# mLSTM attention and two feed-forward layers: heads 4 to 7 with their batch halves swapped, the state's part of the output in the scores' burst, output in the pair banks, new planner offsets

## The chip, the cores and the metric

The kernel runs on one core of a Trainium2 chip. The metric is the time in device microseconds of one execution; several runs are taken and their median is compared. The engines are PE (matrix products; PEld is its weight load), DVE (VectorE), ACT (ScalarE), POOL (GpSimd) and SP (which issues the DMAs).

## The reference

Inputs: q, k, v and the output gate of shape (4 batches, 8 heads, 768 steps, 40), input and forget gates (4, 8, 768). All is computed in float32.

```
for t in range(S):                      # mLSTM, for each batch b and head h
    m_new = max(f[t] + m, i[t])
    f_s, i_s = exp(f[t] + m - m_new), exp(i[t] - m_new)
    C = f_s * C + i_s * outer(v[t], k[t])
    n = f_s * n + i_s * k[t]
    y[t] = sigmoid(o[t]) * (C @ q[t]) / max(abs(n . q[t]), 1)
x = y as (3072, 320)
x = leaky(x @ w_in1) @ w_out1           # 320 -> 2048 -> 320, slope 0.01
x = h * cos(h), h = x @ w_in2; out = that @ w_out2
```

## The kernel before

**Attention.** The 768 steps are cut into 12 spans of 64 (T), the four batches into two pairs, which gives 24 chunks in the order `ORDER` (span s, pair p). A chunk holds two batches (j = 0, 1), each on 64 of the 128 partitions, and 8 heads, h = 4 hh + a. `pair` is a PSUM tile of two banks. `a_scores` (L554) writes k times q into it: contraction over the 40 features on rows 64 hh, output rows 64 j, bank hh. `a_weigh` (L561) multiplies with the decay weights, which `a_scan` (L533) makes. `a_out` then issues three groups: q times the state into `pair` (L575, only for s > 0), weights times v into `po` (L583, contraction over the 64 steps on rows 64 j, output rows 64 j) and the state's update into `pair` (L591). `a_ys` (L619, L621) scales the state's part and adds it to `po`; `a_norm`, `a_scale` and `a_gate` (L642) make the chunk's output x from it. `po` is a bank of the ring `acc` (three banks) for chunks 0 to 3 and of the ring `tr` (one bank) afterwards. `a_kt` (L543) scales k for the update; `a_scores` is queued behind it. `g_turn` (L322, L327) turns the gates of several spans from rows to columns by small matmuls with the identity.

**Feed-forward.** Layer 0 runs over 8 blocks of 4, 2, 3, ... chunks of 128 tokens, layer 1 over 8 blocks of 3; each block has 16 slots, one for each 128 of the 2048 hidden features. A slot is 8 matmuls in (L710), an activation, a split into high and low parts (`gh`, `gl` at L758) and 3 matmuls per chunk out (L778). x is turned by the PE (`x_turn`, L469). Block 0 needs all of chunks 0 to 3. The weights arrive as 64-bit words (704 KB each) and are decoded: `w_bits` (L386), `w_round` (POOL), `w_mask` (L402), `w_hi` (ACT), `w_lo` (L417).

**Order.** A planner, `Schedule.run`, issues all work. Each task has a due time (`t_need` of the chunk or `t_slot` of the slot, less an offset from `OFF`), a cost, tasks that it depends on, and rings of buffers that it takes and frees; of the tasks that can start first on an engine it picks the one with the earliest due time. The resulting order is what each engine's queue holds; the planner's times aren't used on the chip. `g_busy` (L251) issues dummy matmuls in the first part.

Of the kernel before, what the change touches and what calls it, by code (L numbers as in the profile page):

```python
# [10 lines left out]
F32 = mybir.dt.float32  # L11
# [11 lines left out]
P = 128  # L23
# [13 lines left out]
KV = OO + DM  # L37
O_S, O_C = HD * E1, 2 * HD * E1
SR = T + D
# [11 lines left out]
SLOW = 50.0  # L51
T_START = 16.163
ATT_LEAD = 25.402
BACKLOG = 0.429
HORIZON = 180.0
ATT_GAP = 11.301
ATT_STEP = 13.206
OUT_LAG = 6.451
SLOT0 = 2.559
DEC_LEAD = 35.272  # L60
BUSY = [-1.11, 44.0, 0.7, -11.9]
SPREAD = 4
# [106 lines left out]
def mlstm_moe(ctx, tc, qk, kvo, ig, fg, w1, w2, const, out):  # L169
# [145 lines left out]
    def g_turn(eng, c0, c1):  # L315
        pt = bank() if c0 < 4 else tps.tile([P, 512], F32, tag="tr", name="pt")
        pt = pt[:, :(c1 - c0) * 6 * H]
        pt = pt_t[c0] = pt.rearrange("p (s k n) -> p s k n", k=3, n=2 * H)
        for s in range(c0, c1):
            for k, t in enumerate((gt["i"], gt["m"])):  # L320
                for j in range(2):
                    nc.tensor.matmul(  # L322
                        pt[T * j:T * j + T, s - c0, k, :].rearrange("p (b h) -> p b h", h=H), t[:, s * T:s * T + T],
                        ident[:BH, :BH].rearrange("r (b j h) -> r j b h", j=2, h=H)[:, j], start=True, stop=True, skip_group_check=True,
                    )
        for hh in range(2):
            nc.tensor.matmul(pt[T * hh:T * hh + T, :, 2, :], ones, pick[:, hh, c0:c1, :], start=True, stop=True, skip_group_check=True)  # L327

# [285 lines left out]

    def a_ys(eng, c):
        s, p = ORDER[c]
        y = ap.tile([P, 2, HD, E1], F32, tag="y", name="y", bufs=1)
        g = col[:, s, 1, p * H:(p + 1) * H].rearrange("p (k a) -> p k a", k=2).unsqueeze(3)
        nc.vector.tensor_tensor(y, s_ps.rearrange("p k (a e) -> p k a e", e=E1), g.to_broadcast([P, 2, HD, E1]), ALU.mult)  # L619
        po = at[c]["po"]  # L620
        nc.vector.tensor_tensor(po, po, y.rearrange("p k a e -> p (k a e)"), ALU.add)  # L621

    def a_norm(eng, c):
        if eng == "ACT":
            at[c]["d"] = ap.tile([P, H, 1], F32, tag="d", name="d")
        d = at[c]["d"]
        n = at[c]["po"].rearrange("p (h e) -> p h e", e=E1)[:, :, D:E1]
        if eng == "ACT":
            nc.scalar.activation(d, n, AF.Abs)
# [9 lines left out]
    def a_gate(eng, c):  # L639
        o = at[c]["kvo"][:, OO:].rearrange("p (h d) -> p h d", d=D)  # L640
        x = ap.tile([P, H, D], F32, tag="x", name="x")
        nc.vector.tensor_tensor(x, at[c]["po"].rearrange("p (h e) -> p h e", e=E1)[:, :, :D], o, ALU.mult)  # L642
        ax[c] = x.rearrange("p h d -> p (h d)")

    def plan_attention(n, c, j, m):
        s, p = ORDER[c]
        e = t_need[c]
        last, k = s == NS - 1, (0, c)
        c0 = max(c for c, _ in TURNS if c <= s)
# [16 lines left out]
        if not last:  # L666
            kt = [("kt", c)]
            sch.add(("kt", c), e - OFF["kt"], [pool(DM), dve(DM)], a_kt, c, deps=[("kvo", c), ("scan", c)])
        sch.add(("s", c), e - OFF["s"], ("PE", 0.72), a_scores, c, deps=[("qk", c, 0), ("qk", c, 1), ("scan", c), "clear"] + kt,
                take=[("p", (c, 0), (s > 0) + (not last)), ("p", (c, 1), (s > 0) + (not last))])  # L670
        sch.add(("weigh", c), e - OFF["weigh"], dvp(4 * P), a_weigh, c, deps=[("s", c), ("scan", c)] + kt)
        sch.add(("sig", c), e - OFF["sig"], ("ACT", 0.36), a_sig, c, deps=[("kvo", c), ("exp", 2, "f"), ("exp", 2, "i")], table="sig")
        sch.add(("out", c), e - OFF["out"], ("PE", 1.3 + (0.45 if s else 0) + (0.27 if not last else 0)), a_out, c,
                deps=[("weigh", c), ("vext", c)] + ([("state", c - 2)] if s else []) + kt
                + ([("col", TURNS[-1][0])] if c == BLOCKS1[0] else []),
                take=[(po_ring(c), ("po", c), 1)], free=[("fb", c), ("raw", c), ("kvo", c)])
        if s:
            sch.add(("ys", c), e - OFF["ys"], ("DVE", 0.82), a_ys, c, deps=[("out", c)], free=[("p", (c, 0)), ("p", (c, 1))])
        sch.add(("norm", c), e - OFF["norm"], ("ACT", 0.08), a_norm, c, deps=[("ys", c) if s else ("out", c)], take=[("d", c, 1)])
        sch.add(("rec", c), e - OFF["norm"], ("DVE", 0.3), a_norm, c, deps=[("norm", c)])  # L680
        sch.add(("scale", c), e - OFF["scale"], [pool(DM), dve(DM)], a_scale, c, deps=[("rec", c), ("sig", c)], free=[("d", c)])
        sch.add(("gate", c), e - OFF["gate"], dvp(DM), a_gate, c, deps=[("scale", c)], take=[("x", k, 1)],
                free=[(po_ring(c), ("po", c)), ("kvo", c)])
        if not last:
            if s:
                sch.add(("decay", c), t_need[c - 2] - OFF["decay"], [pool(H * E1), dve(H * E1)], a_decay, c, deps=[("state", c - 2), ("col", c0)],
                        take=[("tmp", c, 1)])
            sch.add(("state", c), e - OFF["state"], dvp(H * E1) if s else [("ACT", 0.35), dvp(H * E1)], a_state, c,
                    deps=[("out", c)] + ([("decay", c)] if s else []), free=[("p", (c, 0)), ("p", (c, 1))] + ([("tmp", c)] if s else []))
        plan_x(0, n, c, j, e - OFF["tr"], ("gate", c), ax, "x", m)  # L690
# [244 lines left out]
```

## Time and profile before

| what | value |
|---|---|
| runs | 830.17, 831.56, 831.58 us; median 831.56 |
| profiled execution | span 829.0 us from first to last instruction; no other time of its own is shown |
| busy | PE 813.4, PEld 781.0, DVE 602.0, ACT 430.8, POOL 85.4 us |
| first layer matmul | 55.25 us |

The span is the time between the first and last instruction of the profiled execution; what an execution spends around it is in the runs' times only. PE's busy time holds its dummy matmuls.

### The profile page before, as it was taken

To read this page: it belongs to the slowest core of one execution; us is meant where nothing else is said; L and a number is where in the kernel's file an instruction comes from. 1 tells how busy PE (TensorE), PEld (TensorE's weight loads), DVE (VectorE), ACT (ScalarE), POOL (GpSimd) and SP (SyncE) were. 2 spreads that over 40 slices of the span, in tenths; PEclk is the share of its full clock that TensorE was granted. 3 is DMA by queue.
4 is the path that set the end of the run, shared out by engine and by line. 5 is a ranking of instruction groups with operands and counts; after the bars stand their busy time and mean duration, and the time that the engine had idled before them with its cause. 6 is when DMAs were issued, how large, how long until landed. Compare 5 with 4: busy or idle time off the path is not lost.

```text
span 829.0 us, 19156 instructions
## 1 busy us (share of the span) xinstructions
PE 813.4 (98%) x7782; PEld 781.0 (94%) x7792; DVE 602.0 (73%) x1250; ACT 430.8 (52%) x925; POOL 85.4 (10%) x68
## 2 busy tenths in 40 slices
PE   7979999999999999999999999999999999999998
PEld 5758889999999999999999999999999999999998
DVE  7888875557465663665517798989898988888885
ACT  3456634443344344443344565656565666666564
POOL 2442311112111121100000000000000000000000
PEclk8599999999999999999999999999999999999999
DMA  8466354535243352643215300000000000010000
GB/s 240 157 206 180 118 144 136 163 119 171 88 156 109 135 167 85 190 127 125 77 51 165 113 25 17 25 25 25 25 25 25 25 17 33 9 32 17 9 17 25
DMA packets 29976, 74.55 MB, mean 90 GB/s; under 512 B 4353, under 2 KB 13697, under 8 KB 29889
## 3 DMA queue, kind: packets, MB, share of 16 engines
q1 hardware_dynamic: 29888, 73.33, 28.5%
q8 instruction: 61, 1.00, 0.5%
q14 instruction: 27, 0.21, 0.1%
HBM read 59.60 MB, written 13.71 MB: 88 GB/s over the span
## 4 chain that ended last, share of the span: by engine, by line
PE 91%; DVE 3%; ACT 0%; issue 0%
PE acc L778 41%; PE ph L710 36%; PE pair L710 6%; PE po L583 2%; PE tr L469 2%; PE pair L554 2%; PE pair L575 1%; DVE w L417 1%; PE pair L591 1%; DVE wf L402 0%; ACT w L199 0%; PE busy L251 0%; DVE r L735 0%; DVE g L746 0%; DVE y L619 0%
## 5 line engine op out<-in xcount | busy, mean ns | idle before, releaser
L778 PE MATMUL acc<-w,gh 128*128 128x320 f32 x1568 | 348.0, 309 | 0.0
L710 PE MATMUL ph<-xt,w 128*128 128x384 f32 (+2 forms) x1760 | 344.1, 338 | 0.1
L710 PEld LDWEIGHTS ph<-xt,w 128*128 128x128 f32 x1760 | 297.2, 188 | 5.7 <-PE busy L251 0.6
L778 PEld LDWEIGHTS acc<-w,gh 128*128 128x128 f32 x1568 | 264.2, 188 | 2.5
L778 PE MATMUL acc<-w,gl 128*128 128x320 f32 (+1 forms) x784 | 238.7, 308 | 0.0
L758 DVE TENSOR_TENSOR gl<-ph,gh 128x384 fp32r<-128x384 f32 (+2 forms) x124 | 68.6, 553 | 115.3 <-ACT ph L719 115.0
L718 ACT ACTIVATE gh<-ph 128x384 fp32r<-128x384 f32 (+2 forms) x124 | 60.9, 491 | 166.9 <-PE ph L710 124.2
L778 PEld LDWEIGHTS acc<-w,gl 128*128 128x128 f32 x784 | 145.9, 188 | 0.3 <-DVE gl L758 0.2
L740 ACT ACTIVATE r<-r,hpi 128x384 f32<-128x384 f32 x128 | 78.9, 616 | 61.9 <-DVE r L736 61.7
L199 ACT CAST gh<-g 128x384 fp32r<-128x384 f32 x128 | 65.7, 513 | 46.1 <-PE acc L778 37.8
L398 POOL TENSOR_TENSOR wf<-wf,raw 128x704 int32<-128x704 int32 x32 | 60.7, 1897 | 270.8 <-DVE wf L386 143.1
L758 DVE TENSOR_TENSOR gl<-g,gh 128x384 fp32r<-128x384 f32 x128 | 70.5, 550 | 5.5 <-ACT gh L199 5.5
L746 DVE TENSOR_TENSOR g<-ph,r 128x384 f32<-128x384 f32 x96 | 53.4, 556 | 15.4 <-ACT r L740 14.1
L719 ACT ACTIVATE ph<-ph 128x384 f32<-128x384 f32 (+2 forms) x124 | 60.3, 486 | 0.0
L710 PE MATMUL pair<-xt,w 128*128 128x384 f32 x288 | 56.1, 337 | 1.1 <-DVE g L746 1.1
L726 ACT ACTIVATE t<-ph 128x384 f32<-128x384 f32 x96 | 47.0, 489 | 17.1 <-PE ph L710 11.2
L735 DVE SCALAR_TENSOR_TENSOR r<-t,ph 128x384 f32<-128x384 f32 x96 | 53.2, 555 | 3.3
L732 DVE TENSOR_SCALAR t<-t 128x384 f32<-128x384 f32 x128 | 45.7, 357 | 12.0 <-ACT t L726 8.4
L710 PEld LDWEIGHTS pair<-xt,w 128*128 128x128 f32 x288 | 49.4, 188 | 1.4 <-DVE g L746 1.4
L736 DVE TENSOR_SCALAR r<-r 128x384 f32<-128x384 f32 x128 | 46.1, 360 | 4.4
L199 ACT CAST xt<-tr 128x256 fp32r<-128x256 f32 x96 | 25.2, 316 | 17.0 <-PE tr L469 17.0
L417 DVE TENSOR_TENSOR w<-wf,w 128x704 fp32r<-128x704 f32 x32 | 32.5, 1016 | 1.7 <-ACT w L199 1.1
(93 smaller groups left out, 666.4 us busy)
## 6 DMA issues: line engine op xcount, KB each, us to landing
raw<-w SPq DMA_DIRECT2D x32, 704.0 KB, 5.9
kvo<-kvo SPq DMA_DIRECT2D x24, 484.0 KB, 4.6
raw<-qk SPq DMA_DIRECT2D x48, 192.0 KB, 4.7
w2d<-wf SPq DMA_DIRECT2D x16, 352.0 KB, 2.5
wf<-w2d SPq DMA_DIRECT2D x16, 352.0 KB, 3.2
fb<-sfd SPq DMA_DIRECT2D x40, 128.0 KB, 3.5
x2d<-o SPq DMA_DIRECT2D x24, 160.0 KB, 1.8
x<-x2d SPq DMA_DIRECT2D x24, 160.0 KB, 2.2
```

Of the source, the lines that this page charges most:

```text
L199: nc.scalar.copy(dst, src)
L398: nc.gpsimd.tensor_tensor(f, f, wraw.pop((l, i))[:, :, 0], ALU.add)
L710: nc.tensor.matmul(ph[:, :N], w[:, a:a + P], x[:, b, :N], start=k == 0, stop=k == 7)
L718: nc.scalar.activation(t["gh"][:, :N], h, AF.Prelu, alpha=0.01)
L719: nc.scalar.activation(h, h, AF.Prelu, alpha=0.01)
L726: nc.scalar.activation(t["a"][:, :N], t["h"][:, :N], AF.Copy, scale=1.0 / TWO_PI, bias=0.25)
L735: nc.vector.scalar_tensor_tensor(r, a, -TWO_PI, t["h"][:, :N], ALU.mult, ALU.add)
L736: nc.vector.tensor_scalar(r, r, -4.712388, 1.5707959, ALU.max, ALU.min)
L740: nc.scalar.activation(r, r, AF.Sin, bias=hpi)
L746: nc.vector.tensor_tensor(t["g"][:, :N], t["h"][:, :N], t["r"][:, :N], ALU.mult)
L758: on[eng].tensor_tensor(t["gl"][:, :N], t["g"][:, :N], t["gh"][:, :N].bitcast(F32), ALU.subtract)
L778: nc.tensor.matmul(po, a[:, s], w[:, b, e], start=i == 0 and k == 0 and j < 3, stop=i == NF - 1 and k == 2, skip_group_check=True,)
```

## The change

In q, k, v and the gates, heads 4 to 7 lie with the two batches of a pair exchanged, so that their steps of batch j stand on the partitions of batch 1 - j; the output gate stays. Matmuls of these heads write to the rows of their true batch. The weights times v go to `ps[hh]`: for chunks 0 to 3 two banks of `acc`, afterwards the two banks of `pair`. The state's part is issued in `a_scores`, to other columns of `pair`, and scaled by a new task `ym`. From chunk 4 on the banks of `pair` are freed by the weighing, the state's update and the gate. Turning the gates takes more and smaller matmuls. The planner's constants are new.

```diff
-O_S, O_C = HD * E1, 2 * HD * E1
+O_C, O_S = HD * E1, 512 - HD * E1
...
-T_START = 16.163
-ATT_LEAD = 25.402
+T_START = 26.475
+ATT_LEAD = 18.152
...
-ATT_GAP = 11.301
-ATT_STEP = 13.206
...
-DEC_LEAD = 35.272
+ATT_GAP = 9.276
+ATT_STEP = 10.696
...
+DEC_LEAD = 34.492
...
 OFF = {
-    "fb": 117.132, "kvo": 14.305, "qk": 13.373, "vext": 0.206, "scan": 113.123, "kt": -27.683, "s": -1.889, "weigh": 134.356, "out": 1.728,
-    "sig": 41.602, "ys": 144.171, "norm": -42.558, "scale": 136.89, "gate": 112.746, "state": 61.378, "decay": 54.572, "tr": 61.443,
-    "x2": 16.215, "l_a": -78.384, "l_g": -57.167, "l_cos": 77.728, "l_mul": 3.513, "l_gh": 58.007,
-    "l_gl": 101.205, "w_round": -66.41, "w_mask": 45.509, "w_hi": -52.232, "w_lo": 103.697, "w_load": -9.735,
+    "fb": 59.294, "kvo": 22.296, "qk": 24.167, "vext": 132.922, "scan": 113.856, "kt": 8.959, "s": 5.345, "weigh": 26.276, "out": -2.716,
+    "sig": 60.18, "ym": 66.406, "ys": 123.389, "norm": 36.865, "scale": 27.072, "gate": 48.573, "state": 80.334, "decay": 116.597, "tr": -11.831,
+    "x2": 16.236, "l_a": 22.842, "l_g": -40.025, "l_cos": 6.259, "l_mul": 80.975, "l_gh": 87.277,
+    "l_gl": -78.065, "w_round": 13.341, "w_mask": 35.707, "w_hi": -24.26, "w_lo": -27.626, "w_load": -7.818,
...
-            for k, t in enumerate((gt["i"], gt["m"])):
-                for j in range(2):
+            for j in range(2):
+                nc.tensor.matmul(
+                    pt[T * j:T * j + T, s - c0, 0, :].rearrange("p (b h) -> p b h", h=H), gt["i"][:, s * T:s * T + T],
+                    ident[:BH, :BH].rearrange("r (b j h) -> r j b h", j=2, h=H)[:, j], start=True, stop=True, skip_group_check=True,
+                )
+            for j in range(2):
+                for hh in range(2):
+                    r = T * (j ^ hh)
                     nc.tensor.matmul(
-                        pt[T * j:T * j + T, s - c0, k, :].rearrange("p (b h) -> p b h", h=H), t[:, s * T:s * T + T],
-                        ident[:BH, :BH].rearrange("r (b j h) -> r j b h", j=2, h=H)[:, j], start=True, stop=True, skip_group_check=True,
+                        pt[r:r + T, s - c0, 1, :].rearrange("p (b k a) -> p k b a", k=2, a=HD)[:, hh], gt["m"][:, s * T:s * T + T],
+                        ident[:BH, :BH].rearrange("r (b j k a) -> r j k b a", j=2, k=2, a=HD)[:, j, hh], start=True, stop=True,
+                        skip_group_check=True,
                     )
-        for hh in range(2):
-            nc.tensor.matmul(pt[T * hh:T * hh + T, :, 2, :], ones, pick[:, hh, c0:c1, :], start=True, stop=True, skip_group_check=True)
+        nc.tensor.matmul(pt[:T, :, 2, :], ones, pick[:, 0, c0:c1, :], start=True, stop=True, skip_group_check=True)
+        for j in range(2):
+            o, i = (x.rearrange("p s (b j a) -> p j s b a", j=2, a=HD) for x in (pt[T:, :, 2, :], pick[:, 1, c0:c1, :]))
+            nc.tensor.matmul(o[:, 1 - j], ones, i[:, j], start=True, stop=True, skip_group_check=True)
...
     def a_scores(eng, c):
+        s, p = ORDER[c]
         r = at[c]["raw"]
+        for a in range(HD if s else 0):
+            for hh in range(2):
+                for j in range(2):
+                    k, o = slice(T * hh, T * hh + D), T * (j ^ hh)
+                    nc.tensor.matmul(
+                        pair[o:o + T, hh, O_S + a * E1:O_S + (a + 1) * E1], r[k, 0, a * P + T * j:a * P + T * j + T],
+                        state[p][k, (j ^ hh) * HD + a, :], start=True, stop=True, skip_group_check=True,
                    )
...
+    def own_po(c):
+        return c < BLOCKS1[0]
+
+    def halves(x):
+        return x.rearrange("p (k h d) -> p k h d", k=2, h=HD)
 
     def a_out(eng, c):
         s, p = ORDER[c]
         t = at[c]
-        po = t["po"] = (bank() if po_ring(c) == "acc" else tps.tile([P, 512], F32, tag="tr", name="po"))[:, :H * E1]
-        if s:
-            for a in range(HD):
-                for hh in range(2):
-                    for j in range(2):
-                        k = slice(T * hh, T * hh + D)
-                        nc.tensor.matmul(
-                            pair[T * j:T * j + T, hh, O_S + a * E1:O_S + (a + 1) * E1],
-                            t["raw"][k, 0, a * P + T * j:a * P + T * j + T], state[p][k, j * HD + a, :],
-                            start=True, stop=True, skip_group_check=True,
-                        )
-        for h in range(H):
-            for j in range(2):
-                r = slice(T * j, T * j + T)
-                nc.tensor.matmul(
-                    po[r, h * E1:(h + 1) * E1], t["w"][r, h, :], t["v"][r, h, :], start=True, stop=True, skip_group_check=True,
-                )
+        if own_po(c):
+            ps = [bank()[:, :HD * E1] for _ in range(2)]
+            t["po"] = [(slice(k, k + 1), x.unsqueeze(1).rearrange("p k (h e) -> p k h e", e=E1)) for k, x in enumerate(ps)]
+        else:
+            ps = [pair[:, k, :HD * E1] for k in range(2)]
+            t["po"] = [(slice(0, 2), pair[:, :, :HD * E1].rearrange("p k (h e) -> p k h e", e=E1))]
+        for a in range(HD):
+            for hh in range(2):
+                for j in range(2):
+                    r, h, o = slice(T * j, T * j + T), hh * HD + a, T * (j ^ hh)
+                    nc.tensor.matmul(
+                        ps[hh][o:o + T, a * E1:(a + 1) * E1], t["w"][r, h, :], t["v"][r, h, :], start=True, stop=True, skip_group_check=True,
+                    )
         if s < NS - 1:
             for a in range(HD):
                 for j in range(2):
                     for hh in range(2):
                         r, h = slice(T * j, T * j + T), hh * HD + a
                         nc.tensor.matmul(
-                            pair[T * hh:T * hh + D, j, O_C + a * E1:O_C + (a + 1) * E1],
+                            pair[T * hh:T * hh + D, j ^ hh, O_C + a * E1:O_C + (a + 1) * E1],
...
-    def a_ys(eng, c):
+    def a_inter(eng, c):
         s, p = ORDER[c]
-        y = ap.tile([P, 2, HD, E1], F32, tag="y", name="y", bufs=1)
+        y = at[c]["y"] = ap.tile([P, 2, HD, E1], F32, tag="y", name="y", bufs=1)
         g = col[:, s, 1, p * H:(p + 1) * H].rearrange("p (k a) -> p k a", k=2).unsqueeze(3)
         nc.vector.tensor_tensor(y, s_ps.rearrange("p k (a e) -> p k a e", e=E1), g.to_broadcast([P, 2, HD, E1]), ALU.mult)
-        po = at[c]["po"]
-        nc.vector.tensor_tensor(po, po, y.rearrange("p k a e -> p (k a e)"), ALU.add)
+
+    def a_ys(eng, c):
+        y = at[c]["y"]
+        for k, po in at[c]["po"]:
+            nc.vector.tensor_tensor(po, po, y[:, k], ALU.add)
 
...
-        sch.add(("s", c), e - OFF["s"], ("PE", 0.72), a_scores, c, deps=[("qk", c, 0), ("qk", c, 1), ("scan", c), "clear"] + kt,
-                take=[("p", (c, 0), (s > 0) + (not last)), ("p", (c, 1), (s > 0) + (not last))])
-        sch.add(("weigh", c), e - OFF["weigh"], dvp(4 * P), a_weigh, c, deps=[("s", c), ("scan", c)] + kt)
+        sch.add(("s", c), e - OFF["s"], ("PE", 0.72 + (0.45 if s else 0)), a_scores, c,
+                deps=[("qk", c, 0), ("qk", c, 1), ("scan", c), "clear"] + kt + ([("state", c - 2)] if s else []),
+                take=[("p", (c, a), 1 + (not own) + (not last)) for a in range(2)])
+        if s:
+            sch.add(("ym", c), e - OFF["ym"], dvp(H * E1), a_inter, c, deps=[("s", c), ("col", c0)], take=[("y", c, 1)])
+        sch.add(("weigh", c), e - OFF["weigh"], dvp(4 * P), a_weigh, c, deps=[("s", c), ("scan", c)] + kt, free=pair_)
...
-        sch.add(("out", c), e - OFF["out"], ("PE", 1.3 + (0.45 if s else 0) + (0.27 if not last else 0)), a_out, c,
-                deps=[("weigh", c), ("vext", c)] + ([("state", c - 2)] if s else []) + kt
+        sch.add(("out", c), e - OFF["out"], ("PE", 0.72 + (0.27 if not last else 0)), a_out, c,
+                deps=[("weigh", c), ("vext", c)] + kt
                 + ([("col", TURNS[-1][0])] if c == BLOCKS1[0] else []),
-                take=[(po_ring(c), ("po", c), 1)], free=[("fb", c), ("raw", c), ("kvo", c)])
+                take=[("acc", ("po", c, a), 1) for a in range(2)] if own else [], free=[("fb", c), ("raw", c), ("kvo", c)])
         if s:
-            sch.add(("ys", c), e - OFF["ys"], ("DVE", 0.82), a_ys, c, deps=[("out", c)], free=[("p", (c, 0)), ("p", (c, 1))])
...
         sch.add(("gate", c), e - OFF["gate"], dvp(DM), a_gate, c, deps=[("scale", c)], take=[("x", k, 1)],
-                free=[(po_ring(c), ("po", c)), ("kvo", c)])
+                free=([("acc", ("po", c, a)) for a in range(2)] if own else pair_) + [("kvo", c)])
...
+    def tiles(x, turned=True):
+        x = x.reshape(B // 2, 2, H, NS, T, -1)
+        return np.concatenate([x[:, :, :HD], x[:, ::-1, HD:]], 2) if turned else x
...
-        return x.reshape(BH, S)
+        return tiles(x).reshape(BH, S)
...
-        "kvo": np.concatenate([tmajor(k), tmajor(ve), tmajor(o)], 2),
+        "kvo": np.concatenate([tmajor(k), tmajor(ve), tmajor(o, False)], 2),
```

## Rows read from the trace of the kernel before

**Rows 1.** The page, part 1: busy us, share of the span, instructions.
```profile
PE 813.4 (98%) x7782; PEld 781.0 (94%) x7792; DVE 602.0 (73%) x1250; ACT 430.8 (52%) x925; POOL 85.4 (10%) x68
```

**Rows 2.** PE's waits from 62 us to the end: us in total, times, longest.
```profile
PE pair L710 <- DVE g L746: 1.1, 1, 1.1
PE tr L469 <- DVE x L642: 0.3, 1, 0.3
```

**Rows 3.** Timeline of PE, 36 to 58 us: start, length, line, tiles, [idle before].
```profile
42.34 0.27 PE L322 MATMUL pt<-ident,scratch 32*64 32x16 f32 x4
42.46 0.27 PE L322 MATMUL pt<-ident,i 32*64 32x16 f32 x4
...
44.15 0.69 PE L554 MATMUL pair<-raw 40*64 40x64 f32 x32
...
48.23 0.50 PE L591 MATMUL pair<-kvo 64*40 64x41 f32 x28
...
55.25 2.20 PE L710 MATMUL ph<-xt,w 128*128 128x512 f32 x8
```

**Rows 4.** Timeline of PE around one chunk, 165 to 171 us.
```profile
165.97 0.69 PE L554 MATMUL pair<-raw 40*64 40x64 f32 x32
166.60 0.56 PE L778 MATMUL acc<-w,gh 128*128 128x320 f32 x2
...
168.62 0.68 PE L575 MATMUL pair<-state,raw 40*64 40x41 f32 x32
169.11 1.04 PE L583 MATMUL po<-kvo,fb 64*64 64x41 f32 x29
169.93 0.23 PE L591 MATMUL pair<-kvo 64*40 64x41 f32 x2
```

**Rows 5.** Busy by stretch, L583 alone, then L575 alone: length, PE, PEld, clock.
```profile
62.00:428.00 366.00, 22.44 (x640) 20.60 (x640) 1.00 0.42 131
...
62.00:428.00 366.00, 13.52 (x640) 11.15 (x640) 1.00 0.42 131
```

**Rows 6.** Timeline of DVE in the start, 20 to 56 us.
```profile
25.89 1.22 DVE L533 TENSOR_TENSOR_SCAN fb<-acc,eye 128x512 f32<-128x512 f32 x1 [0.63 <-PE acc L521]
...
39.36 0.48 DVE L543 TENSOR_TENSOR kvo<-kvo,fb 128x320 f32<-128x320 f32 x1
...
46.08 0.68 DVE L561 TENSOR_TENSOR fb<-pair,fb 128x512 f32<-128x512 f32 x1
...
48.40 2.18 DVE L417 TENSOR_TENSOR w<-wf,w 128x704 fp32r<-128x704 f32 x1 [0.41 <-ACT w L199]
50.50 0.49 DVE L619 TENSOR_TENSOR y<-pair,col 128x328 f32<-128x328 f32 x1
```

**Rows 7.** Timelines of PE and DVE: two of the four close pairs of chunks.
```profile
224.89 0.69 PE L554 MATMUL pair<-raw 40*64 40x64 f32 x32
...
227.91 0.48 DVE L642 TENSOR_TENSOR x<-po,kvo 128x320 f32<-128x320 f32 x1
...
229.64 0.49 PE L469 MATMUL tr<-ident,x 128*128 128x128 f32 x3
...
330.56 0.69 PE L554 MATMUL pair<-raw 40*64 40x64 f32 x32
...
333.99 0.49 PE L469 MATMUL tr<-ident,x 128*128 128x128 f32 x3
```

**Rows 8.** Busy by stretch: PE, PEld, DVE, ACT, POOL, granted clock, DMA, GB/s.
```profile
20.00:25.00 5.00, 5.00 (x90) 3.91 (x89) 4.03 (x15) 1.19 (x4) 2.16 (x2) 0.50 0.58 186
```

**Rows 9.** Timeline of the SP queue in the start.
```profile
31.39 0.43 SPq L502 DMA_DIRECT2D raw<-qk  x1
```

**Rows 10.** The page, part 6: DMA issues, KB each, us to landing.
```profile
raw<-qk SPq DMA_DIRECT2D x48, 192.0 KB, 4.7
```

**Rows 11.** Busy by stretch: the first block, and one block of the last layer.
```profile
55.00:126.00 71.00, 70.66 (x753) 62.27 (x751) 58.88 (x89) 41.78 (x74) 20.50 (x14) 1.00 0.55 161
...
520.00:564.00 44.00, 44.00 (x282) 43.95 (x281) 37.86 (x86) 27.14 (x57) 0.00 (x0) 1.00 0.07 23
```

More of the change, by code (lines that the diff above doesn't have):

```diff
@@ L51 @@
 SLOW = 50.0
-T_START = 16.163
-ATT_LEAD = 25.402
+T_START = 26.475
+ATT_LEAD = 18.152
 BACKLOG = 0.429
 HORIZON = 180.0
-ATT_GAP = 11.301
-ATT_STEP = 13.206
-OUT_LAG = 6.451
-SLOT0 = 2.559
-DEC_LEAD = 35.272
+ATT_GAP = 9.276
+ATT_STEP = 10.696
+OUT_LAG = 5.292
+SLOT0 = 1.076
+DEC_LEAD = 34.492
 BUSY = [-1.11, 44.0, 0.7, -11.9]
@@ L63 @@
 TURNS = [(0, 2), (2, 4), (4, 8), (8, 12)]
-GATES_AT = 18.859
-TURN_LEAD = 20.179
-W2 = {0: -8.486, 1: -26.828}
+GATES_AT = 16.825
+TURN_LEAD = 20.703
+W2 = {0: 14.147, 1: -26.543}
 OFF = {
-    "fb": 117.132, "kvo": 14.305, "qk": 13.373, "vext": 0.206, "scan": 113.123, "kt": -27.683, "s": -1.889, "weigh": 134.356, "out": 1.728,
-    "sig": 41.602, "ys": 144.171, "norm": -42.558, "scale": 136.89, "gate": 112.746, "state": 61.378, "decay": 54.572, "tr": 61.443,
-    "x2": 16.215, "l_a": -78.384, "l_g": -57.167, "l_cos": 77.728, "l_mul": 3.513, "l_gh": 58.007,
-    "l_gl": 101.205, "w_round": -66.41, "w_mask": 45.509, "w_hi": -52.232, "w_lo": 103.697, "w_load": -9.735,
+    "fb": 59.294, "kvo": 22.296, "qk": 24.167, "vext": 132.922, "scan": 113.856, "kt": 8.959, "s": 5.345, "weigh": 26.276, "out": -2.716,
+    "sig": 60.18, "ym": 66.406, "ys": 123.389, "norm": 36.865, "scale": 27.072, "gate": 48.573, "state": 80.334, "decay": 116.597, "tr": -11.831,
+    "x2": 16.236, "l_a": 22.842, "l_g": -40.025, "l_cos": 6.259, "l_mul": 80.975, "l_gh": 87.277,
+    "l_gl": -78.065, "w_round": 13.341, "w_mask": 35.707, "w_hi": -24.26, "w_lo": -27.626, "w_load": -7.818,
 }
@@ L626, in a_norm @@
         d = at[c]["d"]
-        n = at[c]["po"].rearrange("p (h e) -> p h e", e=E1)[:, :, D:E1]
         if eng == "ACT":
-            nc.scalar.activation(d, n, AF.Abs)
+            for k, po in at[c]["po"]:
+                nc.scalar.activation(halves(d.rearrange("p h e -> p (h e)"))[:, k], po[:, :, :, D:E1], AF.Abs)
         else:
@@ L639, in a_gate @@
     def a_gate(eng, c):
[L640 to L643, printed above, removed]
+        x = ax[c] = ap.tile([P, DM], F32, tag="x", name="x")
+        for k, po in at[c]["po"]:
+            nc.vector.tensor_tensor(halves(x)[:, k], po[:, :, :, :D], halves(at[c]["kvo"][:, OO:])[:, k], ALU.mult)
     def plan_attention(n, c, j, m):
@@ L647, in plan_attention @@
         e = t_need[c]
-        last, k = s == NS - 1, (0, c)
+        last, k, own = s == NS - 1, (0, c), own_po(c)
+        pair_ = [("p", (c, 0)), ("p", (c, 1))]
         c0 = max(c for c, _ in TURNS if c <= s)
@@ L675, in plan_attention @@
                 + ([("col", TURNS[-1][0])] if c == BLOCKS1[0] else []),
-                take=[(po_ring(c), ("po", c), 1)], free=[("fb", c), ("raw", c), ("kvo", c)])
+                take=[("acc", ("po", c, a), 1) for a in range(2)] if own else [], free=[("fb", c), ("raw", c), ("kvo", c)])
         if s:
-            sch.add(("ys", c), e - OFF["ys"], ("DVE", 0.82), a_ys, c, deps=[("out", c)], free=[("p", (c, 0)), ("p", (c, 1))])
-        sch.add(("norm", c), e - OFF["norm"], ("ACT", 0.08), a_norm, c, deps=[("ys", c) if s else ("out", c)], take=[("d", c, 1)])
+            sch.add(("ys", c), e - OFF["ys"], ("DVE", 0.5 if own else 0.41), a_ys, c, deps=[("out", c), ("ym", c)], free=[("y", c)])
@@ L680, in plan_attention @@
+        sch.add(("norm", c), e - OFF["norm"], ("ACT", 0.2 if own else 0.1), a_norm, c, deps=[("ys", c) if s else ("out", c)], take=[("d", c, 1)])
         sch.add(("rec", c), e - OFF["norm"], ("DVE", 0.3), a_norm, c, deps=[("norm", c)])
@@ L688, in plan_attention @@
             sch.add(("state", c), e - OFF["state"], dvp(H * E1) if s else [("ACT", 0.35), dvp(H * E1)], a_state, c,
-                    deps=[("out", c)] + ([("decay", c)] if s else []), free=[("p", (c, 0)), ("p", (c, 1))] + ([("tmp", c)] if s else []))
+                    deps=[("out", c)] + ([("decay", c)] if s else []), free=pair_ + ([("tmp", c)] if s else []))
         plan_x(0, n, c, j, e - OFF["tr"], ("gate", c), ax, "x", m)
@@ L893, with tmajor @@
     q, k, v, o = (np.asarray(inputs[n]) for n in ("q", "k", "v", "o_gate"))
-    def tiles(x):
-        return x.reshape(B // 2, 2, H, NS, T, -1)
+    def tiles(x, turned=True):
+        x = x.reshape(B // 2, 2, H, NS, T, -1)
+        return np.concatenate([x[:, :, :HD], x[:, ::-1, HD:]], 2) if turned else x
     def dmajor(x):
         return tiles(x).reshape(B // 2, 2, 2, HD, NS, T, D).transpose(4, 0, 2, 6, 3, 1, 5).reshape(NC, 2, D, HD * P)
-    def tmajor(x):
-        return tiles(x).transpose(3, 0, 1, 4, 2, 5).reshape(NC, P, -1)
+    def tmajor(x, turned=True):
+        return tiles(x, turned).transpose(3, 0, 1, 4, 2, 5).reshape(NC, P, -1)
     def gates(x):
-        return x.reshape(BH, S)
+        return tiles(x).reshape(BH, S)
     ve = np.concatenate([v, np.ones((B, H, S, 1), v.dtype)], 3)
```

5 lines of the change are left out of this document (2 added, 3 removed).

## The prediction, written before the result was known

> **What bounds the kernel now.** I read the page first: TensorE (PE) is busy 813.4 of 829.0 us [rows 1]. A busy PE alone proves little, so the second view was who PE waits for after the start. From 62 us to the end it waited 1.4 us in all [rows 2]; the reader should see that no semaphore, DMA or other engine stands behind the PE list in two entire layers. So from the first layer matmul on, the time is the sum of what PE issues, and only a shorter list shortens it. Before that the picture is another: the first layer matmul starts at 55.25 us [rows 3], and PE fills the time with dummy matmuls. These 55 us are a chain of four attention chunks, through VectorE mostly. I therefore price the change twice: once for the list (20 chunks), once for the start (4 chunks).
>
> The median of the runs shown is 831.56 us and the profiled span 829.0; the sum is made against the span, and the 2.56 us between them are carried over unchanged.
>
> **The output burst.** In one steady chunk [rows 4] PE does three bursts of 32 records each: scores (L554), then the state's part (L575), weights times v (L583) and the state update (L591). The state's part goes from 168.62 to 169.11: 0.49 us, or 15.3 ns a record. The weights-times-v burst next to it, with the same 41 columns, goes from 169.11 to the first L591 at 169.93: 0.82 us, 25.6 ns a record. The difference that I see is in the code: the first visits all four 64x64 quarters of the array (row half hh, column half j), the second only the two on the diagonal (rows r, outputs r). Turning the batch halves of heads 4 to 7 sends their outputs to the other half, so all four quarters are visited. The new burst's price isn't in the trace; its nearest row is L575, equal but for 64 rows of contraction in place of 40. That gives 0.82 - 0.49 = 0.33 us a chunk, 6.6 us over 20. The other reading is by busy time over the same stretch, 22.44 us for L583 against 13.52 for L575 at 640 records each [rows 5]: 8.9 us; it contains overlaps at the seam with L591. I take 7.5, between them. Ends: 0 (the quarters don't overlap) and 8.9.
>
> One row and one rule disagree here. The scores need 0.63 us from their first matmul to the next other one, 0.49 of it for the same 32 records [rows 4], so starts 15 ns apart happen on this chip. The Trainium skill (TensorE: Matmul & The Clock Gate, section "Wait — 56ns, not 53.3ns?") says that starts never come closer than about 25 ns; by it the 25.6 ns would be a floor already and the burst would gain nothing. The row in this very kernel decides for me.
>
> **The state's part moved into the scores' burst.** 32 records leave one burst and enter the other. Two bursts a chunk remain, so the seams stay (0.14 us behind the scores: 166.60 less 165.97 less 0.49 [rows 4]): 0 on PE. It now needs the state of the chunk two earlier sooner than before, by the 2.65 us from scores to output burst; that state is a whole chunk old then, so I price this at 0, and at up to 2.65 us a chunk if it were not. The multiplication y (0.50 us, L619 in [rows 6]) can run before the output burst, so the chain behind that burst gets 0.5 us shorter; layer matmuls lie between the bursts and cover it, so this pays nothing in the list.
>
> **The output moved into the pair banks.** From chunk 4 on the result stays in the two pair banks until the gate multiplication reads it, and the next chunk's scores wait for that. Before, they waited only for y and the state. In the trace one chunk's scores start at 224.89 while the gate of the chunk before runs at 227.91 [rows 7]. Behind the scores the whole PE list would stand. There are four such pairs of chunks in the trace. Two are as this one: the gate ends at 228.39, 3.5 us after the scores' start. Two are as the one at 330.56, where the transpose that waits for the gate comes at 333.99; in the first pair that transpose comes 1.25 us after the gate, so the gate ends 2.2 us after the scores' start. If the planner re-orders them, layer matmuls go first and it costs 0; left in place, the stalls are 3.5, 3.5, 2.2 and 2.2 us, 11.4 in all. I take 0, since the new task list has the gate in the ring that frees the banks and layer matmuls are always there to fill.
>
> **The start.** Extra: each step of the turned gates gets four more records, 0.12 us at full clock (42.34 to 42.46) and twice that at the clock of 0.50, the level of 1.2 GHz, granted from 20 to 25 us and in the three stretches of five us after it [rows 3, 8]; six of the twelve steps lie in each, 2.2 us, plus four more small matmuls, 0.2. All run before 44 us beside dummies. Splitting abs, addition and gate for chunks 0 to 3 adds ten instructions; at an estimated 0.1 us each, a fifth of the whole 0.5 us steps, 1 us. If none of it is covered the start loses 3.4 us. Each of these outputs takes two banks from the ring of three, so an output waits for the gate before it, and the spread gates and turns share one bank; no row shows that wait. In the chain the four chunks follow each other anyway, so I put it at 0, and rival 2 holds the other case.
>
> Gain: what is late in the chain of the fourth chunk [rows 6]. Its scan ends at 27.11, but the k scaling (L543) that the scores need comes only at 39.36, the scores at 44.15 [rows 3, 6]. The cause is readable in the due times: the k scaling stands 27.7 behind the chunk's due time, which is behind the first step of all 16 weight decodes (they begin 35.3 before it and lie one planned slot of 3.9 apart). The new offset puts it 9.0 ahead, in front of every mask step (L402). Then the weighting (L561) starts at 46.08, 1.2 us after the scores' end, and y at 50.50, 1.8 us after the last L591's end at 48.73, since a weight subtraction (L417) of 2.18 us holds VectorE. The SP queue changes too: by the offsets the fourth chunk's q,k loads pass three weight loads that stood before them (704 KB each); the number and size of transfers stay. Upper end of the gain: the second q,k half was issued at 31.39 with a median landing of 4.7 [rows 9, 10], so scores at 36 instead of 44: 8 us. Lower end: a loss of 3.4. VectorE bounds what may follow: it is busy 58.88 of 71 us from 55 to 126 [rows 11], with one decode due in each slot, so not much more can be pulled. I take a gain of 3, the two late starts on VectorE.
>
> **Sum.** 829.0 - 7.5 - 3.0 = 818.5 us of span; with 2.56 outside it 821.1 us.
>
> **Rivals.** A change under 0.2% (1.7 us) can't be told from none here.
> 1. The start gains its whole 8 us: 816.1. For it: the chain rows; against: VectorE's load in the first block. 0.17; own range 811 to 818.
> 2. The start loses 3.4: 829.0 - 7.5 + 3.4 + 2.56 = 827.5. For it: three output banks shared by six users; against: the dummies beside them. 0.13.
> 3. The change doesn't do what it says: a record costs 25 ns whatever quarter it visits, only the start gains: 828.6. Against it the 15 ns of scores and state. This is what the rule above would do; 0.04.
> 4. The four scores stay where they are and wait for the gates: 821.1 + 11.4 = 832.5. For it: the dependence is new and lies on the bounding queue; against: matmuls to put between. 0.07; no change.
> 5. The other side: the new due times disturb layer 1. There VectorE is busy 37.9 of 44 us in a block of 16 slots while PE is full [rows 11], so a slot has 0.38 us to spare. If the last step before PE (gl, L758) queues behind one more 0.556 us step in each slot, it is 0.17 late, and 128 slots give 22 us: 843. From 0.1 us a slot on the kernel is slower than before. Against it: before, the whole layer had one wait of 1.1 us. 0.08.
>
> **Numbers.** The forecast case has 0.5 (818 to 825). Faster holds it and rivals 1 to 3: 0.84; no change 0.08 (rival 4 and its neighbours); slower 0.08. For the range I leave out rivals 4 and 5 and the far end of 1: 812 to 831.
>
> **What would show it.** Right: L583's successor, from first record to the first L591 at 0.5 us; no waits of PE after the start; first layer matmul at about 52 us. Wrong: 0.8 us for that burst; PE rows at the scores that wait for the gate (x from pair); gaps at the layer matmuls of layer 1 ended by DVE; a first layer matmul later than 58 us, or one before 48 with gaps behind it that wait for w.

## The result, and the profile after

The changed kernel takes 821.17 us (median of 4 runs, 820.07 to 821.96), the kernel before 830.87 beside it: ratio 0.9884, interval 0.987 to 0.9899. The profiled span went from 829.0 to 820.0. The time of the forecast is met, but not by its terms. What follows the first layer matmul gave 8.7 us where 7.5 were taken (9.2 less of work in PE's list, 0.5 more of waiting), and the start gave 0.3 where 3 were taken. The remaining 0.7 of the 9.7 us is no property of the kernel: the profiled execution after took 821.81 us, 0.6 more than the median. In every profiled run below, the time is 1.7 to 1.9 us longer than the span.

The page's first part; it answers to [rows 1]:

```profile
PE 805.8 (98%) x7837; PEld 773.0 (94%) x7848; DVE 601.9 (73%) x1256; ACT 429.3 (52%) x932; POOL 83.1 (10%) x65
```

PE lost 7.6 us of busy time (its dummy matmuls included), POOL 2.3, ACT 1.5 and VectorE 0.1. Two stretches of PE's timeline, an output burst and the scores with the state's part ahead of them (start, length, line, tiles), and from the kernel before the row that follows those of [rows 4]:

```profile
330.39 0.68 PE L600 MATMUL pair<-kvo,fb 64*64 64x41 f32 x32
330.88 0.50 PE L608 MATMUL pair<-kvo 64*40 64x41 f32 x32
331.31 0.56 PE L801 MATMUL acc<-w,gh 128*128 128x320 f32 x2
...
182.56 0.68 PE L563 MATMUL pair<-state,raw 40*64 40x41 f32 x32
183.05 0.67 PE L572 MATMUL pair<-raw 40*64 40x64 f32 x32
183.65 1.14 PE L733 MATMUL ph<-xt,w 128*128 128x384 f32 x5
...
170.47 0.56 PE L778 MATMUL acc<-w,gh 128*128 128x320 f32 x2
```

Each of these small matmuls of the code leaves two records. Weights times v (L600) go from 330.39 to 330.88: 0.49 us for 32 records, 15.3 ns each, where they took 0.82. The update (L608) behind them needs 0.43 up to the next layer matmul; before it was 0.54 (from 169.93 in [rows 4] to the layer matmul at 170.47). From the first record of the output burst to the next layer matmul that is 0.92 us in place of 1.36. The state's part takes its 0.49 in its new place.

PE's busy time by stretch for L600 alone (length, PE, PEld, clock, DMA), beside the first row of [rows 5]:

```profile
62.00:428.00 366.00, 13.52 (x640) 11.15 (x640) 1.00 0.44 139
```

13.52 against 22.44: 8.92 us, to the digit what L575 had promised. PE's waits from 40 us to the end (total, times, longest), as [rows 2]:

```profile
PE tr L478 <- DVE x L662: 3.9, 1, 3.9
PE acc L801 <- DVE gl L781: 0.9, 1, 0.9
PE ph L733 <- DVE gl L781: 0.6, 1, 0.6
...
PE tr L478 <- DVE g L769: 0.4, 1, 0.4
```

The first lies in the start; behind the first layer matmul PE waits 1.9 us in all. No wait of the scores for the gate is among them. One of the close pairs shows why, on PE and then on DVE:

```profile
227.53 0.68 PE L600 MATMUL pair<-kvo,fb 64*64 64x41 f32 x32
228.02 0.50 PE L608 MATMUL pair<-kvo 64*40 64x41 f32 x32
234.06 0.68 PE L563 MATMUL pair<-state,raw 40*64 40x41 f32 x32
```

```profile
232.91 0.48 DVE L662 TENSOR_TENSOR x<-pair,kvo 128x320 f32<-128x320 f32 x1
```

The scores' burst starts 6.5 us after the output burst and 0.67 after the gate's end, layer matmuls in between; in [rows 7] the scores came before the gate. Layer 1 is as it was (a block by stretch, beside [rows 11]):

```profile
520.00:564.00 44.00, 44.00 (x282) 43.95 (x281) 37.55 (x86) 27.06 (x57) 0.00 (x0) 1.00 0.08 23
```

The start, PE's timeline (last column: idle before, and what ended it), beside [rows 3]:

```profile
34.87 0.77 PE L608 MATMUL pair<-kvo 64*40 64x41 f32 x32
36.11 0.40 PE L321 MATMUL pt<-ident,i 32*64 32x16 f32 x4 [0.47 <-PE pair L608]
36.34 0.57 PE L328 MATMUL pt<-ident,scratch 32*64 32x8 f32 x8
...
38.26 0.57 PE L328 MATMUL pt<-ident,scratch 32*64 32x8 f32 x8
38.69 0.34 PE L333 MATMUL pt<-scratch,ones 32*64 32x64 f32 x1
38.70 0.40 PE L336 MATMUL pt<-scratch,ones 32*64 32x32 f32 x2
38.83 0.31 PE L333 MATMUL pt<-scratch,ones 32*64 32x64 f32 x1
38.91 0.40 PE L336 MATMUL pt<-scratch,ones 32*64 32x32 f32 x2
39.77 1.09 PE L563 MATMUL pair<-state,raw 40*64 40x41 f32 x32 [0.47 <-issue]
40.65 1.11 PE L572 MATMUL pair<-raw 40*64 40x64 f32 x32
...
51.84 0.87 PE L478 MATMUL tr<-ident,x 128*128 128x128 f32 x3 [3.95 <-DVE x L662]
54.97 2.19 PE L733 MATMUL ph<-xt,w 128*128 128x512 f32 x8
...
66.80 2.05 PE L733 MATMUL ph<-xt,w 128*128 128x512 f32 x8
```

The scores of chunk 3 begin 3.5 us earlier than in [rows 3] (40.65, 44.15), the first layer matmul 0.28 us earlier; the row at 66.80 is the fourth slot, which is needed further down. Between chunk 2's output and chunk 3's scores stand 3.2 us of turning (36.11 to 39.3), at a granted clock of 0.50, the lower level, and no dummy is among them.

### The profile page after: what moved, and what is told of

Same layout as the page of the kernel before. It is cut to its first block, busy times and chain, and to the rows that moved or that the text cites. A ratio compares the mean times of both kernels' runs of the same rounds, so it can differ in the third digit from the quotient of the medians.

```text
span 820.0 us, 19230 instructions
## 1 busy us (share of the span) xinstructions
PE 805.8 (98%) x7837; PEld 773.0 (94%) x7848; DVE 601.9 (73%) x1256; ACT 429.3 (52%) x932; POOL 83.1 (10%) x65
## 4 chain that ended last, share of the span: by engine, by line
PE 93%; DVE 4%; issue 1%; ACT 1%; ACTq 0%; DVEq 0%
PE acc L801 40%; PE ph L733 35%; PE pair L733 6%; PE busy L251 2%; PE tr L478 2%; PE pair L563 2%; PE pair L572 2%; PE pair L600 1%; PE pair L608 1%; DVE r L758 1%; DVE gl L781 1%; DVE g L769 1%; PE acc L530 1%; DVE t L755 0%; DVE fb L542 0%
## 5 line engine op out<-in xcount | busy, mean ns | idle before, releaser
L426 DVE TENSOR_TENSOR w<-wf,w 128x704 fp32r<-128x704 f32 x31 | 30.4, 981 | 3.0 <-ACT w L199 2.6
```

## The experiments

All were timed beside the kernel before (830.99 to 831.23 us). The list is the span less the first layer matmul's start, less PE's idle time behind that start; the idle time stands by itself. "First layer matmul" is its start in the profiled execution.

| run | median us | ratio, 95% | span | first layer matmul | list | idle |
|---|---|---|---|---|---|---|
| before | 830.87 | | 829.0 | 55.25 | 772.4 | 1.4 |
| after | 821.17 | 0.987-0.9899 | 820.0 | 54.97 | 763.2 | 1.9 |
| e1_old_offsets | 827.72 | 0.9937-0.9975 | 825.4 | 57.95 | 763.2 | 4.2 |
| e2_new_offsets | 826.96 | 0.9944-0.997 | 824.2 | 47.38 | 773.6 | 3.2 |
| e3_two_quarters | 826.44 | 0.9923-0.9953 | 825.0 | 55.30 | 767.9 | 1.8 |
| e4_state_moved | 838.33 | 1.0044-1.0095 | 839.2 | 60.37 | 774.1 | 4.7 |
| e5_pair_always | 824.66 | 0.9907-0.9947 | 829.2 | 61.74 | 764.8 | 2.7 |
| e6_acc_tr | 823.98 | 0.9896-0.994 | 823.3 | 50.99 | 771.2 | 1.1 |
| e7_acc_h | 831.45 | 0.9992-1.0013 | 827.6 | 60.68 | 764.6 | 2.4 |
| e8_acc_h_tr | 832.23 | 1.0008-1.0029 | 830.0 | 65.69 | 763.1 | 1.2 |
| e9_turn_late | 825.56 | 0.9925-0.996 | 824.0 | 53.08 | 765.3 | 5.7 |
| e10_perm | 820.13 | 0.9861-0.9896 | 818.3 | 48.62 | 764.9 | 4.8 |
| e11_perm_late48 | 819.68 | 0.9827-0.9897 | 820.1 | 51.07 | 765.3 | 3.7 |
| e12_scan_behind_gl | 819.66 | 0.9841-0.9874 | 818.4 | 48.65 | 766.1 | 3.7 |

Apart from e10 and e12, the times missed what was expected of them: e1, e2 and e11 fell between the ranges of the two theories, e3 was 2.6 us under its 829, e4 6 us over its range, and e5 to e9 over every range, e7 and e8 by 10 us. So the theories are judged below by the rows, not by the times. The four runs of e11 spread from 817.19 to 821.96, and its profile is of one near the top.

**First question: the four quarters (theory A) or the planner's constants (theory B)?**

e1, the changed kernel with the constants of before:

```diff
-T_START = 26.475
+T_START = 16.163
...
-    "fb": 59.294, "kvo": 22.296, "qk": 24.167, "vext": 132.922, "scan": 113.856, "kt": 8.959, "s": 5.345, "weigh": 26.276, "out": -2.716,
+    "fb": 117.132, "kvo": 14.305, "qk": 13.373, "vext": 0.206, "scan": 113.123, "kt": -27.683, "s": -1.889, "weigh": 134.356, "out": 1.728,
...
```

> The changed kernel with the planner offsets of before (the new task ym gets the offset of ys). Theory A, the four quarters of the array pay: the list of PE after the first layer matmul is some 9 us shorter than before, as in the changed kernel, and the time is 820 to 824 us, the spread being what the start does. Theory B, the new offsets pay: 829 to 832 us.

e2, the kernel before with the new constants (the same lines the other way):

> The kernel before with the new planner offsets alone. Theory A: 828 to 834 us, no shorter list. Theory B: 821 to 824 us.

e3, the changed kernel, whose output burst visits one diagonal pair of quarters, then the other:

```diff
-        for a in range(HD):
-            for hh in range(2):
+        for hh in range(2):
+            for a in range(HD):
                 for j in range(2):
```

> The changed kernel with one loop order turned in the output burst: first all heads of one half, then of the other, so that matmuls next to each other alternate between two quarters of the array as before; the same matmuls, banks, waits and offsets. Theory A: the burst takes 0.8 to 0.9 us in place of 0.49, and the time is 821.2 + 20 x 0.4 = 829 us. Rival, the new place of the output and the shared bursts pay: 821 us and a burst of 0.49.

e4, the kernel before with only the state's part moved into the scores' burst:

```diff
     def a_scores(eng, c):
...
+        if s:
+            for a in range(HD):
+                for hh in range(2):
+                    for j in range(2):
...
+                            t["raw"][k, 0, a * P + T * j:a * P + T * j + T], state[p][k, j * HD + a, :],
...
     def a_out(eng, c):
...
-        if s:
-            for a in range(HD):
-                for hh in range(2):
-                    for j in range(2):
...
-                            t["raw"][k, 0, a * P + T * j:a * P + T * j + T], state[p][k, j * HD + a, :],
```

> The kernel before with the state's part moved into the scores' burst and its scaling in a task of its own, nothing else; old offsets, ym with that of ys. My step says 0 on PE: 829.5 to 832 us, the out burst shorter by 0.49 and the scores' burst longer by as much. Rival, the move saves a drain inside the output burst: 20 chunks x 0.1 to 0.2 us, 827 to 829 us.

The list falls to 763 us with the new structure whichever constants it has (after, e1), and not with the constants alone (e2). e1 has as many attention bursts as the kernel before, 83, which makes it the clean reading: from a burst's first record to the next layer matmul they add up to 50.78 us against 59.83, so 9.05 us, 0.45 a chunk of 2.46. In e3 the same records cost more by their order alone, on PE's timeline:

```profile
333.85 0.76 PE L600 MATMUL pair<-kvo,fb 64*64 64x41 f32 x26
...
334.56 0.53 PE L608 MATMUL pair<-kvo 64*40 64x41 f32 x28
335.02 0.56 PE L801 MATMUL acc<-w,gh 128*128 128x320 f32 x2
```

From the first record to the next layer matmul it takes 1.17 us (333.85 to 335.02; records of the update already lie between those of the burst), against 0.92 in the changed kernel and 1.36 before. So 0.25 of the 0.44 come back, and the list is 4.7 us longer. The order in which the records follow each other is thus what pays; why two diagonals one after the other are cheaper than one throughout was not tried.

One rival lies close to the quarters, the banks of PSUM: before, the whole burst wrote one bank, now `hh` chooses the bank together with the pair of quarters, and e3 changes the order of both. The rows of the turning in the start (38.26 to 39.3, shown above) bear on it, since all of it goes to the one bank `pt`. The matmuls of L328 go to both halves of the columns, and 8 records start in 0.43 us (38.26 to 38.69), 54 ns each. Those of L336 all go to one half, and two records take 0.21 us (38.70 to 38.91), 105 ns each. So within one bank the parts of the array that are visited set the pace. These tiles are smaller (32 rows) and the granted clock was 0.50; whether the second bank adds anything in the output burst, no run shows.

In e4 the bursts sum to 59.71 against 59.83: the moved state's part costs PE nothing. The kernel is slower all the same, by its start (60.37) and by waits for gl (2.9 us at the out matmuls); its profiled execution is 2.6 us above its median.

The start is where the constants act: 55.25 to 47.38 in the old structure, 57.95 to 54.97 in the new one. So theory B holds for the start, and the new structure costs it 2.7 us with the old constants (57.95 against 55.25) and 7.6 with the new (54.97 against 47.38).

**Second question: what in the new structure eats the start, the two output banks a chunk (theory C) or VectorE's load (D)?**

e5 puts the outputs of chunks 0 to 3 into the pair banks, too:

```diff
     def own_po(c):
-        return c < BLOCKS1[0]
+        return False
```

> The changed kernel with the outputs of chunks 0 to 3 in the pair banks too, none in the ring acc. Theory C, the two acc banks of these outputs eat the start that the new offsets give to the kernel before (first layer matmul at 47.4): the banks are free now, but the next chunk's scores wait for the gate instead; first layer matmul at 50 to 58 us, 817 to 824 us. Theory D, what eats it is the load of VectorE and the extra turning: 54 to 56 us, 821 us.

e6, e7 and e8 take the second bank from another ring; `second(c)` gives `tr` in e6, `h` in e7, `h` and `tr` by turns in e8:

```diff
-            ps = [bank()[:, :HD * E1] for _ in range(2)]
+            r2 = second(c)
+            b2 = bank() if r2 == "acc" else (hps if r2 == "h" else tps).tile([P, 512], F32, tag=r2, name="po")
+            ps = [x[:, :HD * E1] for x in (bank(), b2)]
```

> The changed kernel with one of the two banks of chunks 0 to 3 taken from the ring tr in place of acc. One output still waits for the gate before it, and transposes share that bank. Theory C, if the shared acc banks count: first layer matmul 2 to 4 us earlier, 817 to 819 us; if the wait of an output for the gate before it counts: as the changed kernel, 821 us. Theory D: 821 us.

> As the run with tr, but the second bank comes from the ring h (two banks, one of them held by the dummy matmuls). An output waits for the gate before it here too. Theory C: 817 to 821 us; theory D: 821 us.

> The second bank of chunks 0 and 2 from the ring h, of chunks 1 and 3 from tr, so that no output has to wait for the gate of the chunk before and acc is used as in the kernel before. Theory C: the start of the kernel before with the new offsets comes back, first layer matmul at 48 to 51 us, and with the list of the changed kernel 813 to 817 us. Theory D: 820 to 822 us.

None gains, and none is clean. In e6 the first layer matmul comes 4 us earlier, but two turnings (54.70 to 57.8 and 71.88 to 73.6) now stand behind it, in the list, and the first two groups of layer matmuls take 3.78 us each at a granted clock of 0.50, where 2.1 is usual. In e7 and e8 the dummies hold the ring `h`, so an output stands behind all of them (chunk 2's in e8 from 44.43). The profiled execution of e5 took 830.94 us, 6.3 more than its median, and its rows aren't read. Theory C is neither shown nor excluded.

**Third question: is it the turning on PE's path (theory E), or VectorE (D)?**

e9 holds the turning of spans 8 to 11 back until chunk 3's output:

```diff
-                    deps=[("exp", g, "i"), ("pick", c0, 0), ("pick", c0, 1), "zero"], take=[(ring, ("pt", c0), 1)],
+                    deps=[("exp", g, "i"), ("pick", c0, 0), ("pick", c0, 1), "zero"] + ([("out", 3)] if c0 in (8,) else []), take=[(ring, ("pt", c0), 1)],
```

> The changed kernel with the turning of the gates of spans 8 to 11 held back until the output burst of chunk 3 is issued. In the changed kernel it stands in front of chunk 3's scores, from 36.1 to 39.3 us, and VectorE's next steps wait for those scores. Theory E, turning on the path eats the start: chunk 3's scores 3 us earlier, first layer matmul at 51.5 to 53, 817.5 to 819.5 us. Theory D, VectorE's load: 820 to 822 us.

e10 makes a permuted copy of the identity once, so that turning takes no more matmuls than before the change:

```diff
+    turned = cp.tile([BH, BH], F32, name="turned")
...
+            for n, (t, e) in enumerate(((gt["i"], ident), (gt["m"], turned))):
+                for j in range(2):
                     nc.tensor.matmul(
-                        pt[r:r + T, s - c0, 1, :].rearrange("p (b k a) -> p k b a", k=2, a=HD)[:, hh], gt["m"][:, s * T:s * T + T],
...
+                        pt[T * j:T * j + T, s - c0, n, :].rearrange("p (b h) -> p b h", h=H), t[:, s * T:s * T + T],
+                        e[:BH, :BH].rearrange("r (b j h) -> r j b h", j=2, h=H)[:, j], start=True, stop=True, skip_group_check=True,
```

> The changed kernel with a second identity whose columns are permuted (three small copies on POOL), so that the turned gates need as many matmuls as before the change (4 records fewer for each of 12 spans, one matmul fewer for each turn). Theory E: the two turnings ahead of chunk 3's scores get 1 us shorter each, first layer matmul at 53 to 54.5, 819 to 820.5 us. Theory D: 821 us.

e11 is e10 with the turnings of spans 4 to 7 and 8 to 11 held back as in e9 (`c0 in (4, 8)`):

> Permuted identity, and the turnings of spans 4 to 7 and 8 to 11 both held back until chunk 3's output burst. Theory E: 4 to 5 us earlier than in the changed kernel, 815.5 to 818 us, if the turnings fit in the wait behind that burst; theory D: 820 to 822 us.

e12 is e10 with two scans behind the first gl of block 0:

```diff
-                deps=([("fb", c)] if c < SPREAD else [("fb", c, 0), ("fb", c, 1)]) + [("eye", 0), ("eye", 1)],
+                deps=([("fb", c)] if c < SPREAD else [("fb", c, 0), ("fb", c, 1)]) + [("eye", 0), ("eye", 1)] + ([("gl", (0, 0, 0))] if c in (4, 5) else []),
```

> The permuted identity as in the run before, and in addition the scans of chunks 4 and 5, which block 0 doesn't need, stand behind the first gl of block 0. Theory (what the earlier start gains is given back in VectorE's queue, by gl behind two scans of 1.2 us and a weight subtraction): the first layer matmul stays near 48.6 us, PE's 3.7 us of waits for gl shrink to about 1.3, and the time is 816 to 818.5 us. Rival (VectorE's whole load in block 0 sets the pace, and the order of its steps doesn't matter): the waits turn up at later slots of block 0, some 3 to 4 us again, and the time stays between 819.5 and 821 us. A result in between would say that both hold in part.

e9 moves the turning alone: the first layer matmul comes at 53.08, 1.9 us earlier and as theory E expected, yet the time is 825.56, 4.4 us longer. The permuted identity (e10) brings the first layer matmul from 54.97 to 48.62: 6.35 of the 7.6 us, where E expected 0.5 to 2. That isn't the shorter turning alone, since the planner's order changes with it: chunk 2's output burst starts at 28.62 in place of 33.99, and the last turning stands behind chunk 3's scores (33.18). Yet the span shrinks by 1.7 only. PE's timeline of e10, and below it VectorE's:

```profile
48.62 2.12 PE L732 MATMUL ph<-xt,w 128*128 128x512 f32 x8 [0.90 <-ACT xt L200]
...
53.39 0.56 PE L800 MATMUL acc<-w,gh 128*128 128x320 f32 x2 [0.25 <-ACT gh L740]
57.61 0.63 PE L800 MATMUL acc<-w,gl 128*128 128x320 f32 x1 [3.66 <-DVE gl L780]
...
60.84 2.75 PE L732 MATMUL ph<-xt,w 128*128 128x512 f32 x8
65.38 2.05 PE L732 MATMUL ph<-xt,w 128*128 128x512 f32 x8
```

```profile
52.37 1.22 DVE L541 TENSOR_TENSOR_SCAN fb<-fb,eye 128x512 f32<-128x512 f32 x1
53.51 2.33 DVE L425 TENSOR_TENSOR w<-wf,w 128x704 fp32r<-128x704 f32 x1
55.76 1.21 DVE L541 TENSOR_TENSOR_SCAN fb<-fb,eye 128x512 f32<-128x512 f32 x1
56.90 1.26 DVE L780 TENSOR_TENSOR gl<-ph,gh 128x512 fp32r<-128x512 f32 x2
```

The first out matmuls wait 3.66 us for gl, which stands behind two scans for a later block and a weight subtraction. In this pause the clock falls; e10 by stretch (PE, PEld, DVE, ACT, POOL, granted clock):

```profile
50.00:55.00 5.00, 3.64 (x15) 2.08 (x13) 5.00 (x6) 3.17 (x7) 2.41 (x1) 1.00 0.47 153
55.00:60.00 5.00, 2.39 (x10) 2.39 (x10) 4.39 (x6) 1.88 (x3) 1.36 (x2) 0.55 0.53 184
60.00:65.00 5.00, 5.00 (x25) 4.50 (x25) 2.17 (x3) 1.57 (x4) 0.96 (x1) 0.76 0.61 190
```

From the first to the fourth slot of block 0 (48.62 to 65.38) e10 needs 16.8 us, the changed kernel 11.8 (54.97 to 66.80): of 6.35 us ahead 1.4 are left, and 1.7 at the end. In e9 the same wait is 4.2 us, in e11 2.8. e12 moves the scans, and on PE one reads:

```profile
55.73 0.64 PE L800 MATMUL acc<-w,gl 128*128 128x320 f32 x1 [1.75 <-DVE gl L780]
...
58.97 3.61 PE L732 MATMUL ph<-xt,w 128*128 128x512 f32 x8
64.36 2.05 PE L732 MATMUL ph<-xt,w 128*128 128x512 f32 x8
...
109.78 0.45 PE L800 MATMUL acc<-w,gh 128*128 128x320 f32 x2
111.01 0.42 PE L800 MATMUL acc<-w,gl 128*128 128x320 f32 x1 [0.77 <-DVE gl L780]
```

The first wait for gl halves, and the fourth slot comes 1.0 us earlier than in e10 (64.36, 65.38). But at 111 us PE waits for gl again, and from there e12 runs level with e10. VectorE is full ahead of that wait; e12 by stretch:

```profile
95.00:110.00 15.00, 15.00 (x205) 13.28 (x203) 14.97 (x22) 9.34 (x17) 4.72 (x3) 1.00 0.68 188
```

14.97 of 15 us, where e10 has 12.62. The time, 819.66, is what the rival of that run expected. So the order of VectorE's queue caused half of the first wait, and what a better order gained was lost again at a point where VectorE was full. That its load as such did this is argued, not shown: two of its steps there are longer than usual (a scan 2.76 us in place of 1.2, a mask step 2.28 in place of 0.88), and why isn't known. E is right that turning on PE's path delays the first layer matmul, D about what an earlier one is worth. e10, e11 and e12 have the lowest medians, but their intervals overlap that of the changed kernel, so none is shown to beat it.

## Why the prediction came out, step by step

- **What bounds the kernel: right.** e2 starts the list 7.9 us earlier, and its list is not shorter (773.6 against 772.4); only the new structure, with its output burst, shortens it.
- **The output burst: mechanism right, size 1.5 us too small.** Taken were 7.5 us, 0.375 a chunk between two readings. Measured are 9.05 (e1), 0.45 a chunk: 0.33 in L583's successor, as the first reading had it, and 0.11 in the update behind it. What the prediction called overlaps at the seam in the busy times of [rows 5] was time that PE loses, so the reading of 8.9 was the one to take, and 9.05 lies just past the upper end. The prediction gave the quarters as the only difference between its two rows; L575 also writes two banks where L583 writes one. Its price holds either way, and that the quarters count is shown by the rows of the turning only for smaller tiles.
- **Row against rule: the row decided rightly.** 32 records started 15.3 ns apart in a burst that had 25.6 before. The Trainium skill (TensorE: Matmul & The Clock Gate, section "Wait — 56ns, not 53.3ns?") puts the least distance of two starts near 25 ns; the trace agrees with that figure only for the burst on one diagonal, and not for the other bursts of 32 records in a chunk. Rival 3 is out.
- **The state's part moved: 0 on PE, right** (e4: 59.71 against 59.83 us of bursts). Alone and with the old constants it made the kernel 0.7% slower all the same, through start and waits. No run takes it out of the changed kernel, so whether it is free there isn't shown.
- **The pair banks: 0, right.** The four close pairs were re-ordered: from chunk 5 on every scores' burst starts behind the end of the gate before it, and PE has no wait there. So rival 4 didn't happen. Rival 5 didn't either: behind the first layer matmul PE waits 1.9 us in all.
- **The start: failed.** The step "all run before 44 us beside dummies" is the wrong one. In the changed kernel a turning of 3.2 us stands in PE's queue ahead of chunk 3's scores, with no dummy beside it; the kernel before had one of 2.2 us in that place (from 34.21), without a dummy as well. The additional records of all twelve steps were priced at 2.4 us. Moving that one turning gains 1.9 us at the first layer matmul (e9); doing all of them with fewer matmuls, and with the other order that the planner then finds, gains 6.35 (e10). How the 7.6 us divide between turning, order and banks stays open; the bank wait that was put at 0 is part of that. The gain from the due times was there as well, and larger than taken: 7.9 us (e2), where rival 1 named 8. So what rivals 1 and 2 name both happened, the loss at twice rival 2's 3.4, and the two nearly cancelled.
- **What the start is worth: overlooked.** The sum counted each microsecond of the start as one of the time. In e2 7.9 us at the first layer matmul were 4.8 in the span, with 1.8 more of waits behind it. In e10 6.35 were 1.7, since block 0 then waits on VectorE and runs in part at the lower clock. [rows 11] had VectorE's number (58.88 of 71 us), and the text used it only against a larger gain.

So the sum met the time by luck, as its errors offset each other. The list gave 1.2 us more than taken and the start 2.7 less, so the span came out 1.5 longer than forecast (820.0, 818.5). The 2.56 us that were carried over as time outside the span were the median of the three runs then known less the span of another execution; the like difference after is 1.17, which took 1.4 back.

## What to carry to other kernels

Where small tiles fill only part of the array, look at which quarters neighbouring matmuls visit: here laying out the data so that four quarters take turns (and with them two PSUM banks) saved 0.45 us of 2.46 a chunk, and a second order of the same records lost half of it. When two readings of one price differ by "overlap at the seam", measure from burst to next work, not inside the burst. An earlier start is worth only what the engine behind it can deliver: before counting it, look at how full the other engines are just after the point that is to move.

## What was not expected of the hardware

- The same 32 records of 41 columns and the update behind them, up to the next layer matmul, cost 0.92 us over four quarters in turn, 1.17 over two diagonals one after the other, 1.36 over one diagonal (there in one bank).
- In one bank, at a granted clock of 0.50, records to two halves of the columns started 54 ns apart, records to one half 105 ns (L328 and L336 of the changed kernel, 38.26 to 39.3).
- A pause of PE can cost more than its length. In e10 a wait of 3.66 us led to two stretches at granted clocks of 0.55 and 0.76, and a group of eight layer matmuls that takes 2.05 us took 2.75; in e12, with a shorter wait (1.75), 3.61. Not every pause does: in the kernel before PE is busy only 2.02 of the 5 us ahead of the first layer matmul, and the granted clock is 1.00 there and behind it [rows 11]:

```profile
50.00:55.00 5.00, 2.02 (x11) 0.94 (x10) 3.78 (x10) 2.12 (x6) 1.42 (x1) 1.00 0.71 197
```

- Joining transposes and output into one burst (71 bursts in place of 83 in e1) left the list as long as it was (763.2 us in both). That the seams change their place and not their sum is the likely reading; the constants differ between the two as well.
